# A decode attention block with an MLP on one core: the stream of keys and values issued by GpSimd instead of SyncE

## The chip, the core and the metric

The kernel runs on one core of a Trainium2 chip. A core has TensorE (PE) for matrix products, VectorE (DVE), ScalarE (ACT), GpSimd (POOL), and SyncE (SP), which computes nothing and here issues transfers. Each engine has its own list of instructions; semaphores order them against each other and against the 16 DMA engines that move data between HBM and the on-chip memory (SBUF). The metric is the device time of one execution in microseconds (us), the median over runs; lower is better.

## The reference

One token for each of B = 4 sequences. Block A is attention against a cache of 4096 positions, 32 heads of 128 dimensions; block B is a small MLP. Both take the layer-normed input, and both results are added to `x`:

```python
xn = _layernorm(x)
# A: q = xn @ wq; B=4, H=32, Sk=4096, Dh=128
scores = jnp.einsum("bhqd,bhkd->bhqk", q, k_cache) * (Dh ** -0.5)
p = _softmax(scores, axis=-1)
o = jnp.einsum("bhqk,bhkd->bhqd", p, v_cache)      # then o @ wo
# B: with one position the spatial shifts give zeros, so x1 = xn
h2 = _gelu(_layernorm(x1) @ w3) @ w4
return x + A(xn) + (x1 + h2)
```

All data are float32. The key cache and the value cache have 4 * 32 * 4096 * 128 numbers each, 268 MB each; every one is used once.

## The kernel before

**Tiles.** The 128 pairs (sequence, head) are handled in `NJ = 32` groups of four. One group's keys are one tile of 128 partitions x 16384 floats, 8,388,608 bytes: partition p holds 128 consecutive positions of one head, which is one contiguous run of 64 KB in HBM. Values have the same form. There are two tiles for keys (`ks[0]`, `ks[1]`, used in turn) and a single one for values (`vs`); together they take most of SBUF. They also serve other data before and after the loop: `vs` holds `w3` and scratch at the start and `w4` at the end, `ks[1]` holds `wq` at the start, `ks[0]` the last group's values, and `ks[1]` `wo` at the end.

**The three loops.** They run at the same time, one on each engine, and are tied by semaphores.

- DVE, L309 to L338: for each group, wait for its keys, multiply the tile with the query (L329), add up over the 128 dimensions (L330), in two halves of 64 columns, then take the maximum (L335 to L337). After each half it adds 1 to `summed`, so group j is through with its keys at `summed` = 2j + 2.
- ACT, L343 to L356: exponentials of the scores (L348), two copies out of PSUM (L353, L355). The second copy adds 1 to `done`; after that the group's values are no longer needed.
- PE, L375 to L394: wait for the values, multiply them with the exponentials (L382), then two small products (L387, L389).

**The transfers.** `load` (L164) issues a transfer on an engine's list, SP unless told otherwise, after waiting for what frees its target. In program order SP has: `w3`, `wq`, the first keys; keys 1 once the query product has read `wq` (L275); values 0 once three steps of the preamble are through (L276); keys 2 in two halves as the first keys are used up (L277); then in turn values j + 1 after `done` = j + 1 and keys j + 2 after `summed` (L279 to L282); at the end the last values, `w4` (L284), and `wo` in seven pieces (L285 to L292). SP waits in this order, so a transfer is never issued ahead of the one before it on the list. All of them go into one hardware queue (q1 in the profile).

**Handing over a landing.** A transfer adds 16 to its semaphore: `k0`, `k1` or `landed`. The loops' bodies are the same code in every pass, so the reader waits for 16 and takes 16 off again (`take`, L294):

```python
def take(engine, sem, n=1):
    engine.wait_ge(sems[sem], n)
    engine.sem_inc(sems[sem], -n)
```

Keys 2 come in two halves, which would add 16 twice; they land on `half0` and `half1`, and GpSimd waits for both and adds 16 to `k0` (L301, L302). Beside that GpSimd does small work: constants at the start (L185 to L196), clearing `pw` (L265), preparing `g4` near the end (L303, L304), and clearing the semaphores.

**The end.** The last values, `w4` and the pieces of `wo` have semaphores of their own, for which PE waits directly (L399, L402, L415, L433). `wo`'s pieces get smaller (rows of 32, 16, 8, 4, 2 and twice 1 KB per partition), so that PE has little left when the last lands. SP and ACT store the two halves of the result (L441).

Of the kernel before, what the change touches and what calls it, by code (L numbers as in the profile page):

```python
# [88 lines left out]
def decode_block(ctx: ExitStack, tc: tile.TileContext, x, k, v, wq, wo, w3, w4, out):  # L89
    nc = tc.nc  # L90
    B, H, S, DH = k.shape
# [3 lines left out]
    NF = F // P  # L95
# [6 lines left out]
    WC = H * DH // P  # L102
    LAST = NJ - 1

    def sb(name, *shape):
        return nc.alloc_sbuf_tensor(name, [P, *shape], F32).ap()
# [4 lines left out]
    ks = [sb(f"ks{n}", R * DH) for n in range(2)]  # L111
    vs = sb("vs", R * DH)
# [10 lines left out]
    gT = sb("gT", NF, B)  # L123
# [17 lines left out]
    kf = k.rearrange("b h s d -> (b h s d)")  # L141
    vf = v.rearrange("b h s d -> (b h s d)")

    def rows(flat, j):
        n = G * S * DH
        return flat[j * n:(j + 1) * n].rearrange("(p n) -> p n", p=P)

    def blocks4(start, stop, w, m, src):

        for t in range(4):  # L150
            i = nc.tensor.matmul(total[32 * t:32 * t + m, :], w, src[:, P * t:P * t + P], start=start, stop=stop)  # L151
        return i

    do = Steps(nc)
    wo_sems = [nc.alloc_semaphore(f"wo{n}") for n in range(7)]
    sems = {n: nc.alloc_semaphore(n) for n in (
        "x", "w3", "wq", "k0", "k1", "landed", "last", "w4", "go", "pv", "copied", "poz",
        "half0", "half1", "nm", "dve", "summed", "expd", "done", "bye", "out")}
    wo_sb = ks[LAST % 2].rearrange("p (c n) -> p c n", c=WC)
    wo_cuts = ((0, 16), (16, 24), (24, 28), (28, 30), (30, WC - 1))  # L160
    w4_sb = vs[:, :NF * D].rearrange("p (m n) -> p m n", m=NF)
    g4 = vs[:, NF * D:NF * D + 4 * 32].rearrange("p (m i) -> p m i", m=4)

    def load(o, i, sem, by, *after, queue="SP"):  # L164
        return do(queue, lambda e: e.dma_start(o, i), *after, done=(sems[sem], 16, by))
# [22 lines left out]
        out=ident, in_=ident, compare_op=ALU.not_equal, fill=1.0, base=0, pattern=[[-1, P]],  # L188
# [42 lines left out]
    total_ok = do("PE", lambda e: blocks4(False, False, ident[:B, 0:32], 32, xn))  # L231
# [4 lines left out]
    for c in range(NC):  # L236
        for t in range(4):
            up = lambda e: e.matmul(y[32 * t:32 * t + 32, :FT], x1nT[:, c, :], w3_sb[:, c, t * FT:(t + 1) * FT],
                                    start=(c == 0), stop=(c == NC - 1))
            d = do("PE", up)  # L240
# [3 lines left out]
    d = do("DVE", lambda e: e.tensor_mul(u, hs, hs), a)  # L244
    d = do("DVE", lambda e: e.tensor_scalar(u, u, GELU_B, 1.0, op0=ALU.mult, op1=ALU.add), d)
    d = do("DVE", lambda e: e.tensor_mul(u, u, hs), d)
    a = do("ACT", lambda e: e.activation(th, u, AF.Tanh, scale=GELU_A), d)
    d = do("DVE", lambda e: e.tensor_scalar(th, th, 1.0, 0.5, op0=ALU.add, op1=ALU.mult), a)
    d = do("DVE", lambda e: e.tensor_mul(hs, hs, th), d)
    d = do("DVE", lambda e: e.transpose(gt, hs), d)  # L250
    gT_ok = do("DVE", lambda e: e.tensor_copy(gT, gt.rearrange("p (m i) -> p m i", i=32)[:, :, 0:B]), d)
# [4 lines left out]
    for c in range(NC):  # L256
        for n in range(2):
            for h in range(G):
                q = lambda e: e.matmul(pq[n][HP * h:HP * h + HP, :], xnT[:, c, :], wq_h[:, c, n, h],
                                       start=(c == 0), stop=(c == NC - 1))  # L260
                pq_ok = do("PE", q)
    for n in range(2):
        a = do("ACT", lambda e: e.mul(pw_row[:, n * 4 * DH:(n + 1) * 4 * DH], pq[n], DH ** -0.5), pq_ok)  # L263
    d = do("DVE", lambda e: e.transpose(wide, pw_row), a)  # L264
    pw_ok = do("POOL", lambda e: e.memset(pw, 0.0), d)  # L265
    qT_ok = do("DVE", lambda e: e.tensor_copy(
        qT.rearrange("p (b i) n -> p b i n", b=B),
        wide.rearrange("p (i n m) -> p m i n", n=DH // HP, m=32)[:, 0:B]), d)
# [3 lines left out]
    SUMMED = [(sems["summed"], 2 * j + 2) for j in range(NJ)]  # L272
    DONE = [(sems["done"], j + 1) for j in range(NJ)]
    HALF = R * DH // 2
    load(ks[1], rows(kf, 1), "k1", None, pq_ok)  # L275
    load(vs, rows(vf, 0), "landed", None, gT_ok, qT_ok, total_ok)  # L276
    parts = [load(ks[0][:, n:n + HALF], rows(kf, 2)[:, n:n + HALF], f"half{i}", 16, (sems["summed"], i + 1))  # L277
             for i, n in enumerate((0, HALF))]
    for j in range(LAST - 1):  # L279
        if j > 0:  # L280
            load(ks[j % 2], rows(kf, j + 2), f"k{j % 2}", None, SUMMED[j])
        load(vs, rows(vf, j + 1), "landed", None, DONE[j])  # L282
    last_in = load(ks[(LAST - 1) % 2], rows(vf, LAST), "last", 16, SUMMED[LAST - 1])
    w4_in = load(w4_sb, w4.rearrange("(p m) n -> p m n", m=NF), "w4", 16, DONE[LAST - 1])  # L284
    do.wait("SP", [SUMMED[LAST]])  # L285
    wo_r = wo.rearrange("(p c) n -> p c n", c=WC)
    for (c0, c1), sem in zip(wo_cuts, wo_sems):
        nc.sync.dma_start(wo_sb[:, c0:c1], wo_r[:, c0:c1]).then_inc(sem, 16)  # L288
    half = D // 2
    for n, sem in enumerate(wo_sems[-2:]):  # L290
        n *= half
        nc.sync.dma_start(wo_sb[:, WC - 1, n:n + half], wo_r[:, WC - 1, n:n + half]).then_inc(sem, 16)  # L292

    def take(engine, sem, n=1):  # L294

        engine.wait_ge(sems[sem], n)
        engine.sem_inc(sems[sem], -n)  # L297


    nc.gpsimd.sem_inc(sems["expd"], 2)  # L300
    do.wait("POOL", parts)  # L301
    nc.gpsimd.sem_inc(sems["k0"], 16)  # L302
    d = do("POOL", lambda e: e.memset(g4, 0.0), DONE[LAST - 1])  # L303
    g4_ok = do("POOL", lambda e: e.tensor_copy(g4[:, :, 0:B], gT[:, 0:4, :]), d, gT_ok)  # L304


    do.wait("DVE", [qT_ok])
# [1 line left out]
    with nc.Fori(0, NJ // 2, engines=OrderedEngineSet([DVE]), head_slot={DVE: 192}) as j:  # L309
        e, n = nc.vector, 0  # L310
# [8 lines left out]
        for s in range(2):  # L319
# [14 lines left out]
            rm, nm = small[:, s, 0:1], small[:, s, 1:2]  # L334
# [8 lines left out]
    with nc.Fori(0, NJ // 2, engines=OrderedEngineSet([ACT]), head_slot={ACT: 160}) as j:  # L343
        for s in range(2):
            take(nc.scalar, "nm")
            for h in range(G):
                hp = slice(HP * h, HP * h + HP)
                i = nc.scalar.activation(  # L348
                    pw[hp, :, 4 * h:4 * h + 4], sc[s][hp, :].rearrange("p (g w) -> p g w", w=4), AF.Exp,
                    bias=small[hp, s, 1:2], scale=1.0, accum_out=rs[hp, h:h + 1])  # L350
# [45 lines left out]
    for b in range(B - 1):  # L396
        d = do("PE", lambda e: e.matmul(xb[:, b, :], lts[:, b].rearrange("p h q -> p (h q)"), sel, start=True, stop=True),
               LTS[b])
# [4 lines left out]
    for m in range(NF):  # L403
        t, g, n = (m, g4[:, m, :], 32) if m < 4 else (m % 4, gT[:, m, :], B)
        nc.tensor.matmul(y[32 * t:32 * t + n, :], g, w4_sb[:, m, :], start=(m < 4), stop=False)
    d = do("PE", lambda e: e.matmul(xb[:, B - 1, :], lts[:, B - 1].rearrange("p h q -> p (h q)"), sel, start=True,
                                    stop=True), LTS[B - 1])
# [6 lines left out]
    for (c0, c1), sem in zip(wo_cuts, wo_sems):  # L414
        do.wait("PE", [(sem, 16)])  # L415
        for c in range(c0, c1):
            if c < 24:
                t = (c + 2) % 4
                i = nc.tensor.matmul(y[32 * t:32 * t + B, :], X[:, c, :], wo_sb[:, c], start=False, stop=(c >= 20))
            else:  # L420
                i = blocks4(False, False, X[:, c, :], B, wo_sb[:, c])
        d = do("PE", lambda e: i)
# [8 lines left out]
    for t in range(4):  # L431
        q = slice(32 * t, 32 * t + B)
        do.wait("PE", [(wo_sems[5 + t // 2], 16)])  # L433
        d = do("PE", lambda e: e.matmul(total[q, :], X[:, WC - 1, :], wo_sb[:, WC - 1, P * t:P * t + P],  # L434
                                        start=False, stop=True))
# [42 lines left out]
```

## Time and profile before

| what | value |
|---|---|
| median of 3 runs | 1303.03 us (1302.62 to 1303.13) |
| span of the profiled execution, first to last instruction | 1301.2 us |
| DVE, PE, ACT, POOL busy | 1164.4, 370.9, 93.6, 2.5 us |
| transfers of keys, of values | 33 issues (one in halves), 32 issues |

The profile is that of one execution, and its times are counted from the first instruction. The 1.8 us between span and median lie outside the instructions. A "busy" engine is one with an instruction running. For DMA the page gives, in 40 slices of the span, the mean busy share of the 16 DMA engines and what they moved, and for each queue the time its packets took as a share of 16 engines' span. "SPq" is an instruction of SP that issues a transfer; its time is that of issuing alone. A wait put down to "DVEq L297" is one that ended with the engine's own `take`, which follows a landing or another engine's signal.

### The profile page before, as it was taken

What the parts mean: (1) busy time and instruction counts of PE and PEld (TensorE: products, weight loads), DVE (VectorE), ACT (ScalarE), POOL (GpSimd) and SP (SyncE); (2) the same over time, 40 slices, a digit from 0 to 9 for tenths busy, and PEclk for the clock granted to TensorE, in tenths of its full rate; (3) what the DMA queues carried; (4) which work ended last, traced back from release to release, by engine and by line L of the source; (5) the groups of instructions that cost most, each with busy time, mean ns of one, the idle gap of its engine ahead of it and who ended that gap; (6) DMA issues with size and microseconds to landing.
All of it is one profiled execution on the core that took longest, in us unless ns stands there. A gap on an engine that the chain in (4) does not pass through costs nothing. (4 is left out here: it accounts for less than half of the span.)

```text
span 1301.2 us, 6686 instructions
## 1 busy us (share of the span) xinstructions
PE 370.9 (29%) x2652; PEld 132.4 (10%) x2652; DVE 1164.4 (89%) x323; ACT 93.6 (7%) x332; POOL 2.5 (0%) x14
## 2 busy tenths in 40 slices
PE   3221233321233321233331133332123332123338
PEld 1000111100011110011110011110001110001112
DVE  3499999999999999999999999999999999999990
ACT  1000000000000000000000000000000000000001
POOL 0000000000000000000000000000000000000000
PEclk9655666655666665666665666665666665566668
DMA  9999999999999999999999999999999999999998
GB/s 404 446 422 448 425 441 427 433 435 425 445 423 445 425 443 425 433 435 427 443 423 445 425 443 427 435 433 429 439 423 447 423 443 427 439 429 433 435 423 372
DMA packets 10830, 561.08 MB, mean 431 GB/s; under 512 B 1212, under 2 KB 1476, under 8 KB 1736
## 3 DMA queue, kind: packets, MB, share of 16 engines
q1 hardware_dynamic: 10808, 561.00, 99.7%
q8 instruction: 3, 0.05, 0.0%
q14 instruction: 3, 0.02, 0.0%
q10 hardware_dynamic: 16, 0.01, 0.0%
HBM read 561.00 MB, written 0.01 MB: 431 GB/s over the span
## 5 line engine op out<-in xcount | busy, mean ns | idle before, releaser
L329 DVE TENSOR_TENSOR ks<-ks,qb 128x8192 f32<-128x8192 f32 x64 | 556.3, 8692 | 59.2 <-DVEq L297 54.2
L330 DVE TENSOR_REDUCE sc<-ks 128x64 f32<-128x8192 f32 x64 | 555.9, 8686 | 2.2
L382 PE MATMUL pv<-vs,pw 128*32 128x512 f32 x1984 | 285.6, 740 | 869.7 <-PEq L297 869.7
L382 PEld LDWEIGHTS pv<-vs,pw 128*32 128x32 f32 x1984 | 78.5, 133 | 1052.2 <-issue 1052.2
L353 ACT COPY os<-pv 128x512 f32<-128x512 f32 x32 | 18.8, 586 | 827.7 <-ACTq L297 827.7
L348 ACT ACTIVATE pw<-sc,small 32x128 f32<-32x128 f32 x128 | 50.9, 398 | 275.2 <-ACTq L297 274.0
L387 PE MATMUL poz<-sel,os 128*128 128x4 f32 x256 | 32.8, 252 | 28.0 <-PEq L297 28.0
L387 PEld LDWEIGHTS poz<-sel,os 128*128 128x128 f32 x256 | 31.0, 191 | 56.1 <-issue 56.1
L348 ACT ACTIVATION_READ_ACCUMULATOR pw<-sc,small 32x1 f32 x128 | 23.5, 184 | 0.0
L436 DVE COPY os<-total 4x128 f32<-4x128 f32 x2 | 0.6, 282 | 15.0 <-PE total L434 15.0
L335 DVE TENSOR_REDUCE small<-sc 128x1 f32<-128x128 f32 x32 | 9.2, 286 | 4.7
L363 DVE RECIPROCAL rz<-oz 128x96 f32<-128x96 f32 (+1 forms) x2 | 1.1, 553 | 13.6 <-ACT oz L355 13.5
L389 PE MATMUL poz<-rs,ones 128*128 128x4 f32 x64 | 11.7, 253 | 0.0
L321 DVE STREAM_TRANSPOSE qb<-qg 128x128 f32<-128x128 f32 x32 | 10.0, 311 | 1.1
L264 DVE STREAM_TRANSPOSE vs<-pw 128x1024 f32<-128x1024 f32 x1 | 1.2, 1245 | 10.4 <-ACT pw L263 10.4
L320 DVE COPY qg<-qT 128x4 f32 x32 | 5.4, 170 | 5.1 <-issue 4.7
L389 PEld LDWEIGHTS poz<-rs,ones 128*128 128x128 f32 x64 | 9.7, 192 | 0.0
L382 PE MATMUL pv<-ks,pw 128*32 128x512 f32 x64 | 9.5, 757 | 0.0
L202 DVE TENSOR_REDUCE lns<-vs 4x1 f32<-4x512 f32 x1 | 0.7, 674 | 9.5 <-DMA vs<-in_A_x_dram 9.5
L355 ACT COPY oz<-poz 128x8 f32 x32 | 5.3, 166 | 50.8 <-ACTq L297 50.8
L215 PE MATMUL pt<-vs,pw 4*128 4x4 f32 x16 | 4.0, 372 | 16.4 <-DVE pw L209 16.4
L336 DVE STREAM_TRANSPOSE tr<-small 128x32 f32<-128x32 f32 x32 | 6.8, 212 | 1.1
(75 smaller groups left out, 78.4 us busy)
## 6 DMA issues: line engine op xcount, KB each, us to landing
ks<-in_A_k_cache_dram SPq DMA_DIRECT2D x2, 4096.0 KB, 26.9
vs<-in_B_w_dram SPq DMA_DIRECT2D x2, 3584.0 KB, 14.1
ks<-in_A_wo_dram SPq DMA_DIRECT2D x1, 4096.0 KB, 21.8
ks<-in_A_wo_dram SPq DMA_DIRECT2D x1, 2048.0 KB, 26.3
ks<-in_A_wo_dram SPq DMA_DIRECT2D x1, 1024.0 KB, 28.3
ks<-in_A_wo_dram SPq DMA_DIRECT2D x1, 512.0 KB, 29.1
ks<-in_A_k_cache_dram SPq DMA_DIRECT2D x31, 42.2
vs<-in_A_v_cache_dram SPq DMA_DIRECT2D x31, 26.8
```

Of the source, the lines that this page charges most:

```text
L320: step(e.tensor_copy(qg, pairs[:, s, bass.ds(j, 1)].rearrange("p o n -> p (o n)")))
L321: step(e.transpose(qb.rearrange("p (n m) -> p n m", m=HP), qg.unsqueeze(2).to_broadcast([P, DH // HP, HP])))
L329: step(e.tensor_tensor(out=kt, in0=kt, in1=qb.unsqueeze(1).to_broadcast([P, w, DH]), op=ALU.mult))
L330: step(e.reduce_sum(sc[s][:, c:c + w], kt, axis=AX.X))
L335: step(e.reduce_max(rm, sc[s], axis=AX.X))
L336: step(e.transpose(tr[s], rm.to_broadcast([P, HP])))
L348: i = nc.scalar.activation(pw[hp, :, 4 * h:4 * h + 4], sc[s][hp, :].rearrange("p (g w) -> p g w", w=4), AF.Exp, bias=small[hp, s, 1:2], sc ...
L353: nc.scalar.copy(os, pv.rearrange("p (m d) -> p m d", m=4)).then_inc(sems["copied"], 1)
L355: nc.scalar.copy(ozs[:, s, :, bass.ds(j, 1)].rearrange("p n o h -> p n (o h)"), poz[:, 0:2 * G].rearrange("p (n h) -> p n h", n=2)).then_i ...
L382: i = nc.tensor.matmul(pv[32 * t:32 * t + 32, :], pw[:, g, :], vt[:, 4 * g:4 * g + 4, :], start=(g < 4), stop=(g >= NG - 4))
L387: nc.tensor.matmul(poz[:, 0:G], os[:, m, :], sel.rearrange("p (h m) -> p m h", m=4)[:, m, 0:G], start=(m == 0), stop=(m == 3))
L389: nc.tensor.matmul(poz[:, G:2 * G], ones.to_broadcast([P, P]), rs, start=True, stop=True).then_inc(sems["poz"], 1)
```

## The change

Every transfer behind the first keys moves from SP's list to GpSimd's. SP issues `w3`, `wq` and keys 0 as before, and from then on only waits for landings and passes them on: `stream` issues on GpSimd with the new semaphores `dk0`, `dk1`, `dlanded`, on which nothing is ever taken off; `tell` makes SP wait until such a semaphore has reached 16 times the number of landings so far, and add 16 to the old `k0`, `k1` or `landed`. DVE's and PE's loops are unchanged and still take from the old ones. Keys 2 are two issues on one semaphore and one `tell` for both, which replaces `half0`, `half1` and GpSimd's wait. The last values, `w4` and `wo` are issued by GpSimd too, and PE waits for them directly as before. GpSimd's two instructions for `g4` stand between `w4` and `wo` now.

```diff
+    nc.gpsimd.sem_inc(sems["expd"], 2)
+    told = {"k0": 0, "k1": 0, "landed": 0}
+
+    def stream(o, i, sem, *after):
+        do.wait("POOL", after)
+        nc.gpsimd.dma_start(o, i).then_inc(sems["d" + sem], 16)
+
+    def tell(sem, n=1):
+        told[sem] += n
+        nc.sync.wait_ge(sems["d" + sem], 16 * told[sem])
+        nc.sync.sem_inc(sems[sem], 16)
+
-    load(ks[1], rows(kf, 1), "k1", None, pq_ok)
-    load(vs, rows(vf, 0), "landed", None, gT_ok, qT_ok, total_ok)
-    parts = [load(ks[0][:, n:n + HALF], rows(kf, 2)[:, n:n + HALF], f"half{i}", 16, (sems["summed"], i + 1))
-             for i, n in enumerate((0, HALF))]
+    stream(ks[1], rows(kf, 1), "k1", pq_ok)
+    stream(vs, rows(vf, 0), "landed", gT_ok, qT_ok, total_ok)
+    for i, n in enumerate((0, HALF)):
+        stream(ks[0][:, n:n + HALF], rows(kf, 2)[:, n:n + HALF], "k0", (sems["summed"], i + 1))
+    for sem in ("k1", "landed"):
+        tell(sem)
+    tell("k0", 2)
     for j in range(LAST - 1):
         if j > 0:
-            load(ks[j % 2], rows(kf, j + 2), f"k{j % 2}", None, SUMMED[j])
-        load(vs, rows(vf, j + 1), "landed", None, DONE[j])
-    last_in = load(ks[(LAST - 1) % 2], rows(vf, LAST), "last", 16, SUMMED[LAST - 1])
-    w4_in = load(w4_sb, w4.rearrange("(p m) n -> p m n", m=NF), "w4", 16, DONE[LAST - 1])
-    do.wait("SP", [SUMMED[LAST]])
+            stream(ks[j % 2], rows(kf, j + 2), f"k{j % 2}", SUMMED[j])
+            tell(f"k{j % 2}")
+        stream(vs, rows(vf, j + 1), "landed", DONE[j])
+        if j < LAST - 2:
+            tell("landed")
+    tell("landed")
+    last_in = load(ks[(LAST - 1) % 2], rows(vf, LAST), "last", 16, SUMMED[LAST - 1], queue="POOL")
+    w4_in = load(w4_sb, w4.rearrange("(p m) n -> p m n", m=NF), "w4", 16, DONE[LAST - 1], queue="POOL")
+    d = do("POOL", lambda e: e.memset(g4, 0.0), DONE[LAST - 1])
+    g4_ok = do("POOL", lambda e: e.tensor_copy(g4[:, :, 0:B], gT[:, 0:4, :]), d, gT_ok)
+    do.wait("POOL", [SUMMED[LAST]])
...
-        nc.sync.dma_start(wo_sb[:, c0:c1], wo_r[:, c0:c1]).then_inc(sem, 16)
+        nc.gpsimd.dma_start(wo_sb[:, c0:c1], wo_r[:, c0:c1]).then_inc(sem, 16)
...
-    nc.gpsimd.sem_inc(sems["expd"], 2)
-    do.wait("POOL", parts)
-    nc.gpsimd.sem_inc(sems["k0"], 16)
```

What this does to the lists of instructions shows best at two places. The first is the start of the stream. Before, it stands on SP's list, right behind the three transfers of the preamble (a row is a line of the kernel, an operation, target and source, size and the semaphores waited for; nPE, nDVE and nPOOL count steps of those engines):

```order
L165 DMA vs<-in_B_w_dram 128x7168
L165 DMA ks<-in_A_wq_dram 128x16384
L165 DMA ks<-in_A_k_cache_dram 128x16384
L181 UNCONDITIONAL_BRANCH
L165 DMA ks<-in_A_k_cache_dram 128x16384 [waits barrier_Pool_Activation_PE_DVE_SP_release,nPE]
L165 DMA vs<-in_A_v_cache_dram 128x16384 [waits nDVE]
L165 DMA ks<-in_A_k_cache_dram 128x8192 [waits summed] x2
L165 DMA vs<-in_A_v_cache_dram 128x16384 [waits done]
```

Now the same transfers stand on POOL's list, behind its own small work:

```order
L194 MEMSET rs 128x4
L195 MEMSET ones 128x1
L196 MEMSET eps 128x1
L265 MEMSET pw 128x1024 [waits nDVE]
L280 DMA ks<-in_A_k_cache_dram 128x16384 [waits nPE]
L280 DMA vs<-in_A_v_cache_dram 128x16384 [waits nDVE]
L280 DMA ks<-in_A_k_cache_dram 128x8192 [waits summed] x2
L280 DMA vs<-in_A_v_cache_dram 128x16384 [waits done]
```

The transfers keep their order and their waits, but keys 1 come behind L265, which waits for a later step of DVE than keys 1 themselves need.

The second place is the end, the last values, `w4` and `wo`. Before, on SP:

```order
L165 DMA ks<-in_A_v_cache_dram 128x16384 [waits summed]
L165 DMA vs<-in_B_w_dram 128x7168 [waits done]
L288 DMA ks<-in_A_wo_dram 128x8192 [waits summed]
L288 DMA ks<-in_A_wo_dram 128x4096
L288 DMA ks<-in_A_wo_dram 128x2048
L288 DMA ks<-in_A_wo_dram 128x1024
L288 DMA ks<-in_A_wo_dram 128x512
L292 DMA ks<-in_A_wo_dram 128x256 x2
L441 DMA out_dram<-os 4x256 [waits nACT,nDVE]
```

Now, on POOL:

```order
L165 DMA ks<-in_A_v_cache_dram 128x16384 [waits summed]
L165 DMA vs<-in_B_w_dram 128x7168 [waits done]
L304 MEMSET vs 128x128
L305 COPY vs<-gT 128x4x4 [waits nPOOL]
L309 DMA ks<-in_A_wo_dram 128x8192 [waits summed]
L309 DMA ks<-in_A_wo_dram 128x4096
L309 DMA ks<-in_A_wo_dram 128x2048
L309 DMA ks<-in_A_wo_dram 128x1024
L309 DMA ks<-in_A_wo_dram 128x512
L313 DMA ks<-in_A_wo_dram 128x256 x2
```

The two instructions for `g4` now stand in the same list as the transfers; SP keeps the store of its half of the result alone.

More of the change, by code (lines that the diff above doesn't have):

```diff
@@ L157, in decode_block @@
         "x", "w3", "wq", "k0", "k1", "landed", "last", "w4", "go", "pv", "copied", "poz",
-        "half0", "half1", "nm", "dve", "summed", "expd", "done", "bye", "out")}
+        "dk0", "dk1", "dlanded", "nm", "dve", "summed", "expd", "done", "bye", "out")}
     wo_sb = ks[LAST % 2].rearrange("p (c n) -> p c n", c=WC)
@@ L291, in decode_block @@
         n *= half
-        nc.sync.dma_start(wo_sb[:, WC - 1, n:n + half], wo_r[:, WC - 1, n:n + half]).then_inc(sem, 16)
+        nc.gpsimd.dma_start(wo_sb[:, WC - 1, n:n + half], wo_r[:, WC - 1, n:n + half]).then_inc(sem, 16)
     def take(engine, sem, n=1):
@@ L297, in take @@
         engine.sem_inc(sems[sem], -n)
-    nc.gpsimd.sem_inc(sems["expd"], 2)
-    do.wait("POOL", parts)
-    nc.gpsimd.sem_inc(sems["k0"], 16)
-    d = do("POOL", lambda e: e.memset(g4, 0.0), DONE[LAST - 1])
-    g4_ok = do("POOL", lambda e: e.tensor_copy(g4[:, :, 0:B], gT[:, 0:4, :]), d, gT_ok)
     do.wait("DVE", [qT_ok])
```

## The prediction

> **What bounds the kernel now.** I read the head of the page first, then the DMA lines, then the stretches of the span, and last the order in time around a few landings. On the head of the page DVE looks like the bound; the DMA lines say otherwise:
>
> ```profile
> PE 370.9 (29%) x2652; PEld 132.4 (10%) x2652; DVE 1164.4 (89%) x323; ACT 93.6 (7%) x332; POOL 2.5 (0%) x14
> DMA  9999999999999999999999999999999999999998
> q1 hardware_dynamic: 10808, 561.00, 99.7%
> ```
>
> DVE is busy 89% of the span and waits now and then; the 16 DMA engines are busy in every slice, and the packets of SP's queue alone fill 99.7% of 16 engines' span. The stretches (span, busy times, granted clock, DMA share, GB/s) show the same rate from end to end:
>
> ```profile
> 46.00:100.00 54.00, 9.39 (x64) 2.57 (x64) 47.94 (x12) 2.01 (x9) 0.00 (x0) 0.55 0.99 428
> 100.00:660.00 560.00, 148.66 (x1046) 53.47 (x1046) 534.74 (x135) 40.62 (x150) 0.00 (x0) 0.61 1.00 434
> 660.00:1220.00 560.00, 152.19 (x1080) 53.96 (x1084) 520.36 (x130) 37.95 (x140) 0.00 (x0) 0.62 1.00 433
> 1297.00:1301.20 4.20, 2.44 (x61) 1.12 (x52) 0.56 (x2) 0.52 (x2) 0.00 (x0) 1.00 0.17 58
> ```
>
> The order in time gives the exact beat. These are the first use of keys 0, and then, near the end, DVE starting on keys (L329) and PE on values (L382) right after their landings, with SP's issues between:
>
> ```profile
> 51.71 8.69 DVE L329 TENSOR_TENSOR ks<-ks,qb 128x8192 f32<-128x8192 f32 x1 [5.53 <-DVEq L297]
> ...
> 1185.21 0.33 SPq L165 DMA_DIRECT2D vs<-in_A_v_cache_dram  x1
> 1189.88 0.33 SPq L165 DMA_DIRECT2D ks<-in_A_k_cache_dram  x1
> 1193.52 8.69 DVE L329 TENSOR_TENSOR ks<-ks,qb 128x8192 f32<-128x8192 f32 x1 [2.00 <-DVEq L297]
> 1212.88 9.65 PE L382 MATMUL pv<-vs,pw 128*32 128x512 f32 x64 [28.05 <-PEq L297]
> 1225.03 0.33 SPq L165 DMA_DIRECT2D vs<-in_A_v_cache_dram  x1
> 1228.57 0.33 SPq L165 DMA_DIRECT2D ks<-in_A_v_cache_dram  x1
> 1232.22 8.69 DVE L329 TENSOR_TENSOR ks<-ks,qb 128x8192 f32<-128x8192 f32 x1 [2.38 <-DVEq L297]
> ```
>
> From keys 0 (51.71) to keys 31 (1232.22) lie 61 transfers, keys 1 to 31 and values 0 to 29. That is 1180.51 / 61 = 19.35 us each, and 1193.52 to 1212.88 to 1232.22 is 19.36 and 19.34. So no transfer of the loop lost any time: 8,388,608 bytes in 19.35 us are 433.5 GB/s, all through. The kernel is one unbroken stream of 561 MB, with about 2 us ahead of it and 2 us behind. DVE needs about 36.4 us a group (1164.4 / 32) against 38.7 for two transfers; PE and ACT need less.
>
> What the stream does next is decided by how early a transfer is issued:
>
> ```profile
> ks<-in_A_k_cache_dram SPq DMA_DIRECT2D x31, 42.2
> vs<-in_A_v_cache_dram SPq DMA_DIRECT2D x31, 26.8
> ```
>
> Keys are issued 42.2 us ahead of landing and values 26.8 (medians). With 19.35 of its own, a values transfer stands 7.4 us in the queue behind other bytes, a keys transfer 22.9. In the rows above, the values issued at 1185.21 go behind keys that land at about 1193.5: 8.3 us of cover.
>
> **The change, part by part.** Removed: 70 or so issues on SP and GpSimd's wait for two halves. Moved: the same transfers, in the same order, behind the same waits, to GpSimd. Added: a wait and an increment on SP between each landing and its reader, and the preparation of transfers by GpSimd instead of SP's hardware queue. Anything that only delays an issue is free until the cover is used up.
>
> *The rate (the term that matters): taken as 0.* No row shows a transfer issued by GpSimd, so the value must be bounded. The same DMA engines move the same rows of 64 KB between the same memories. Downwards, what is left to gain is the 0.3% the queue doesn't fill (3.9 us) and whatever the engines lose at each row. Pieces of `wo` show that loss; PE starts on the one with 16 KB rows, on the one with 8 KB rows, and at the end on the last pieces as they land:
>
> ```profile
> 1293.99 1.90 PE L419 MATMUL y<-ks,X 128*4 128x512 f32 x16 [1.20 <-DMA ks<-in_A_wo_dram]
> 1296.49 1.06 PE L151 MATMUL total<-ks,X 128*4 128x128 f32 x32 [0.61 <-DMA ks<-in_A_wo_dram]
> ...
> 1298.74 0.71 PE L434 MATMUL total<-ks,X 128*4 128x128 f32 x8
> ```
>
> The stream behind keys 0 runs from 51.71 to 1298.74, 1247 us, so 1% of its rate is 12.5 us. The piece with 8 KB rows has 1,048,576 bytes in 2.50 us, where the stream's rate gives 2.42: 0.08 us over 8 rows per DMA engine, some 10 ns a row. A 64 KB transfer has 8 rows per DMA engine too, so losing nothing at a row would save 0.08 us of 19.35, 64 times: 5 us. Together with the gap, the low end is about 1303 - 6 = 1297. Upwards: should GpSimd cut the 64 KB rows, each cut costs those 10 ns again. Two pieces: 64 * 0.08 = 5 us, 1308. Four: 15 us, 1318. Rows of 8 KB throughout: 64 * 7 * 0.08 = 36 us, 1339. I take 0, since the nearest rows are the 61 transfers themselves, which are uniform.
>
> *The issue itself: 0, hidden.* An issue takes SP 0.33 us. A microsecond or two more per issue lies under the 7.4 us of the values' cover and the 22.9 of the keys'. Without cover it would cost 31 us for each microsecond, since values are issued 31 times in the loop. The Trainium skill, "DMA: Bandwidth & Descriptors", section "Specifications", gives about 1 us to the first byte for a transfer from GpSimd against about 0.6 for one from SyncE; by that the 0.4 us are hidden too, and the sum stays the same. No run here shows it yet.
>
> *The relay on SP: 0.* A landing reaches its reader one wait and one increment later, by SP's shortest rows some tenths of a microsecond. Behind SP's wait stand only the next landings, in the order of the stream, so none is held up by a later one. The readers start that much later, so `summed` and `done` come that much later, out of the same 7.4 us of cover. At the end nothing is relayed: PE waits for the last values, `w4` and `wo` directly.
>
> *The start: 0.* Keys 1 now come behind POOL's clearing of `pw`:
>
> ```profile
> 41.79 0.33 SPq L165 DMA_DIRECT2D ks<-in_A_k_cache_dram  x1
> 44.19 1.05 DVE L266 COPY qT<-vs 128x128 f32<-128x128 f32 x1
> 44.21 0.95 POOL L265 MEMSET pw<- 128x1024 f32 x1 [40.20 <-DVE vs L264]
> 45.27 0.33 SPq L165 DMA_DIRECT2D vs<-in_A_v_cache_dram  x1
> ```
>
> So they are issued at 45.2 instead of 41.8; keys 0 land at 51.7. The cover shrinks from 9.9 to 6.5 us, and values 0 follow at once. If GpSimd's first issue took 6 us more than SP's, the stream would begin to stand still; bounds 0 to 3 us, I take 0.
>
> *The end: +0.5.* `w4` is issued at 1263.16, `wo` from 1267.27 on, with one piece after the other:
>
> ```profile
> 1251.58 9.08 PE L382 MATMUL pv<-vs,pw 128*32 128x512 f32 x64 [26.93 <-PEq L297]
> ...
> 1263.16 0.33 SPq L165 DMA_DIRECT2D vs<-in_B_w_dram  x1
> 1263.19 0.20 POOL L303 MEMSET vs<- 128x128 f32 x1 [1218.03 <-ACT oz L355]
> 1263.46 0.20 POOL L304 COPY vs<-gT 128x16 f32<-128x16 f32 x1
> 1267.27 2.50 SPq L288 DMA_DIRECT2D ks<-in_A_wo_dram  x5
> 1269.82 0.90 SPq L292 DMA_DIRECT2D ks<-in_A_wo_dram  x2
> ...
> 1282.81 1.84 PE L405 MATMUL y<-vs 128*32 128x512 f32 x8
> ```
>
> SP needs 3.45 us for the seven. Should GpSimd need three times as long, the last would be issued at 1278. Behind the values that PE starts on at 1251.58 come the last values, `w4` and `wo`'s first piece, 16.3 MB, which keep the DMA engines busy to about 1289. The two instructions for `g4` (0.20 us each) stand behind `w4`'s issue and are needed only at 1282.81 (L405). What can show is the last landing itself, if its completion takes longer from GpSimd's queue: bounds -0.5 to +2, I take +0.5.
>
> Sum: 1301.2 + 0.5 = 1301.7 for the span, and with the 1.8 us around it **1303.5 us**.
>
> **The rivals.** (1) *Faster: the DMA engines lose less between rows or transfers* when GpSimd prepares them. For it: 0.3% unfilled and some 10 ns a row. Against it: 61 transfers at 19.35 us leave little. It gives 1297 to 1300, say 1299. Beside it stands the fit in the same page of the Trainium skill, section "Anatomy of one DMA — SWDGE (gpsimd) path", with 436 GB/s for the part that grows with size: an estimate by it is 0.6% above the 433.5 here, some 7 us less, 1296.
>
> (2) *Slower: the rate falls* because rows are cut, or one of the 16 DMA engines gets its work later than the others and every transfer waits for it. For it: there is no slack in the rate at all; every loss shows in full. Against it: same engines, same bytes. It decides from the first nanosecond: rows in two, 1308; in four, 1318; 8 KB, 1339. The table in the same page, section "Measured (HBM→SBUF, 128 partitions, SWDGE, issued from GpSimd)", has 425 GB/s at its largest size, 2% under the stream here, an estimate of 1328; it disagrees with the fit of rival 1, and no row here decides between them.
>
> (3) *Slower: values are issued too late.* The point from which it counts is 7 to 8 us of delay between `done` and the first byte. One thing in the trace could be that long: an instruction of DVE, if GpSimd could not prepare a transfer beside it.
>
> ```profile
> 178.73 8.69 DVE L329 TENSOR_TENSOR ks<-ks,qb 128x8192 f32<-128x8192 f32 x1
> 180.11 0.17 ACT L355 COPY oz<-poz 128x8 f32 x1 [1.58 <-ACTq L297]
> 180.30 0.33 SPq L165 DMA_DIRECT2D vs<-in_A_v_cache_dram  x1
> ```
>
> These values would be prepared only at 187.42, 7.1 us late; with a microsecond for the issue the stream stops for about half a microsecond, and if every group were hit so, 31 * 0.5 = 15 us, 1319. Against it: most issues fall beside L330 or into gaps. The Trainium skill, "SBUF — State Buffer", section "Who interferes with whom", has a rule against such changes: GpSimd's preparation of transfers waits for DVE's copies in a two-port mode. It clears L329's and L330's kinds of instruction of that, which leaves DVE's copies here, at most 1.05 us long; by the rule the sum stays.
>
> (4) *Slower by a one-off*: the first issue or the end outside the cover, +3 to +5, 1307.
>
> **How the numbers follow.** My forecast, 1300.4 to 1305.6 by itself: 0.34. Rival 1: 0.24. Rival 2: 0.24. Rival 3: 0.10. Rival 4: 0.08. A measurement of this kernel tells about 0.2% (2.6 us) from no change. So faster 0.24, the same 0.34, slower 0.24 + 0.10 + 0.08 = 0.42. The range 1297 to 1326 leaves out the fastest 0.05, and of rivals 2 and 3 what lies above it, rows cut finer than in four or whole microseconds lost per group, 0.13.
>
> **What would show it.** Right: on the new queue, packets of 64 KB (its megabytes over its packets near 52 KB, as on q1 now), values landing 19.35 us apart, DMA share 1.00 from 100 to 1220. Rival 1: the spacing under 19.3. Rival 2: the spacing over 19.4 with the share still at 1.00, or the share under 1.00 with an even spacing. Rival 3: the median from issue to landing of values near 20 us and a DMA share under 1.00 in the loop. Rival 4: a gap before keys 1 or a later start of PE's last steps, with the loop's beat kept. The forecast is wrong if the beat moves by more than 0.04 us.

## The result and the profile after

| | median | lowest to highest | ratio to before, 95% interval |
|---|---|---|---|
| before (8 runs) | 1303.02 us | 1302.57 to 1303.43 | |
| changed (8 runs) | 1306.38 us | 1303.71 to 1306.82 | 1.0024 (1.0015 to 1.0033) |

The change costs 3.4 us, 0.24%. The profiled execution is the fastest of the eight (1303.71 us, span 1302.3); the other seven took 1306.0 to 1306.8. So its trace shows the loss in small, and the first experiment below was made to get a trace of a usual execution.

First what did not change. From the page of the changed kernel, POOL's issues, the queues and the transfers with their median times to landing; from the stretches of the span, the two long ones (busy time of PE, PEld, DVE, ACT and POOL, granted clock, DMA share, GB/s):

```profile
L280 POOL DMA_DIRECT2D vs<-in_A_v_cache_dram x31 | 16.4, 528 | 916.7 <-ACT oz L370 916.7
...
q0 software_dynamic: 10112, 540.55, 96.0%
q1 hardware_dynamic: 440, 20.45, 3.7%
...
vs<-in_A_v_cache_dram POOLq DMA_DIRECT2D x31, 26.7
ks<-in_A_k_cache_dram POOLq DMA_DIRECT2D x30, 41.9
```

```profile
100.00:660.00 560.00, 149.63 (x1070) 53.81 (x1062) 535.89 (x135) 40.64 (x150) 15.82 (x30) 0.62 1.00 433
660.00:1220.00 560.00, 150.08 (x1076) 53.36 (x1080) 520.40 (x129) 37.91 (x140) 14.78 (x28) 0.61 1.00 433
```

GpSimd's queue q0 carries 540.55 MB in 10112 packets, 53.5 KB each (51.9 KB on q1 before): the 64 KB rows are not cut. The rate is 433 GB/s with a DMA share of 1.00, where it was 434 and 433 before. An issue keeps POOL for 0.53 us where SP needed 0.33, and medians from issue to landing moved by 0.1 and 0.3 us.

Now the order in time at the start, where something did change. These rows of the kernel before stand against the rows of the changed kernel below: the issues of keys 1 (only in the second), values 1 and keys 3, DVE's first start on keys 0, and PE's starts on values 1 and values 2.

```profile
102.33 0.33 SPq L165 DMA_DIRECT2D vs<-in_A_v_cache_dram  x1
123.12 0.33 SPq L165 DMA_DIRECT2D ks<-in_A_k_cache_dram  x1
129.20 8.78 PE L382 MATMUL pv<-vs,pw 128*32 128x512 f32 x64 [27.27 <-PEq L297]
167.90 9.90 PE L382 MATMUL pv<-vs,pw 128*32 128x512 f32 x64 [27.80 <-PEq L297]
```

```profile
44.90 0.67 POOL L280 DMA_DIRECT2D ks<-in_A_k_cache_dram  x1
54.09 8.69 DVE L344 TENSOR_TENSOR ks<-ks,qb 128x8192 f32<-128x8192 f32 x1 [8.12 <-DVEq L318]
105.33 0.53 POOL L280 DMA_DIRECT2D vs<-in_A_v_cache_dram  x1 [15.39 <-ACT oz L370]
125.78 0.53 POOL L280 DMA_DIRECT2D ks<-in_A_k_cache_dram  x1 [19.92 <-DVEq L348]
129.39 8.66 PE L397 MATMUL pv<-vs,pw 128*32 128x512 f32 x64 [24.72 <-PEq L318]
169.04 9.31 PE L397 MATMUL pv<-vs,pw 128*32 128x512 f32 x64 [28.86 <-PEq L318]
```

Keys 0 were issued as before, at about 1.7 us, yet they land later. This is their time from issue to landing, in the kernel before and then in the changed one:

```profile
ks<-in_A_k_cache_dram SPq DMA_DIRECT2D x1, 49.9
```

```profile
ks<-in_A_k_cache_dram SPq DMA_DIRECT2D x1, 52.3
```

So DVE starts on them at 54.09 instead of 51.71. Keys 3 follow at 125.78 instead of 123.12, since their tile is free that much later. Values 1 are nearly on time (129.39 against 129.20). But between values 1 and values 2, two transfers later, lie 39.65 us instead of 38.70. From there the beat is the old one. The changed kernel's PE on values 30 near the end (1251.58 before):

```profile
1252.87 3.69 PE L397 MATMUL pv<-vs,pw 128*32 128x512 f32 x20 [27.59 <-PEq L318]
```

From 169.04 to 1252.87 are 56 transfers, 19.35 us each. Values 2 are 1.14 us late, values 30 1.29, and the span is 1.1 us longer. One hiccup of the stream around 128 us makes nearly the whole difference of this execution, and it begins with keys 0 landing late.

### The profile page after: what moved, and what is told of

It is laid out like the page before. It is cut to its first block, busy times and chain, and to the rows that moved or that the text cites. A ratio compares the mean times of both kernels' runs of the same rounds, so it can differ in the third digit from the quotient of the medians.

```text
span 1302.3 us, 6747 instructions
## 1 busy us (share of the span) xinstructions
PE 366.9 (28%) x2652; PEld 131.6 (10%) x2652; DVE 1164.5 (89%) x323; ACT 93.5 (7%) x332; POOL 40.5 (3%) x86
## 3 DMA queue, kind: packets, MB, share of 16 engines
q0 software_dynamic: 10112, 540.55, 96.0%
## 5 line engine op out<-in xcount | busy, mean ns | idle before, releaser
L397 PE MATMUL pv<-vs,pw 128*32 128x512 f32 x1984 | 282.5, 733 | 873.6 <-PEq L318 873.6
L280 POOL DMA_DIRECT2D vs<-in_A_v_cache_dram x31 | 16.4, 528 | 916.7 <-ACT oz L370 916.7
L280 POOL DMA_DIRECT2D ks<-in_A_k_cache_dram x32 | 17.0, 532 | 231.5 <-DVEq L348 231.5
## 6 DMA issues: line engine op xcount, KB each, us to landing
vs<-in_A_v_cache_dram POOLq DMA_DIRECT2D x31, 26.7
```

What stands on the lines that cost most here:

```text
L280: nc.gpsimd.dma_start(o, i).then_inc(sems["d" + sem], 16)
L397: i = nc.tensor.matmul(pv[32 * t:32 * t + 32, :], pw[:, g, :], vt[:, 4 * g:4 * g + 4, :], start=(g < 4), stop=(g >= NG - 4))
```

## The experiments

Theory A was formed from these rows: keys 0 (still on SP's queue) and keys 1 (now on GpSimd's) are served by the DMA engines in turn, so keys 0 land late, DVE starts late, and the first transfers that wait for DVE are issued too late to keep the stream unbroken. Its rivals: (B) each transfer from GpSimd costs a little; (C) SP's relay; (D) the sharing itself loses time, DVE's start does not matter; (E) only GpSimd's queue takes turns with SP's.

### The changed kernel again

> The changed kernel once more, for a profile of one of its usual executions (1306 us; the profiled one took 1303.71 and its span is 1302.3). Theory A, the start: keys 0 (SP's queue) and keys 1 (GpSimd's) share the DMA engines, so keys 0 land at 54 instead of 51.7 us, DVE starts 2.4 us late, and keys 3 are issued so close to the end of values 1 that the DMA engines run dry there, once. Then the spacing of landings is 19.35 us from keys 4 on, as before, and some 3 us are missing between values 1 and keys 3 (19.9 instead of 19.35 in the trace at hand, 22 to 23 here). Theory B, the beat: every transfer prepared by GpSimd costs a little more; then the spacing is 19.39 to 19.41 all through the loop (64 x 0.05 = 3 us). Theory C, the relay: the landings are as before and PE and DVE start later at the end. Time for all: 1306.4.

Measured: 1306.51 us, ratio 1.0026 (1.0015 to 1.0037). The profiled execution took 1306.58, span 1305.0. Its order in time, with the same places as above:

```profile
43.77 0.67 POOL L280 DMA_DIRECT2D ks<-in_A_k_cache_dram  x1
56.51 8.69 DVE L344 TENSOR_TENSOR ks<-ks,qb 128x8192 f32<-128x8192 f32 x1 [11.66 <-DVEq L318]
107.01 0.53 POOL L280 DMA_DIRECT2D vs<-in_A_v_cache_dram  x1 [14.65 <-ACT oz L370]
128.19 0.53 POOL L280 DMA_DIRECT2D ks<-in_A_k_cache_dram  x1 [20.65 <-DVEq L348]
132.20 9.43 PE L397 MATMUL pv<-vs,pw 128*32 128x512 f32 x64 [25.85 <-PEq L318]
171.71 8.45 PE L397 MATMUL pv<-vs,pw 128*32 128x512 f32 x64 [27.95 <-PEq L318]
...
1255.51 4.97 PE L397 MATMUL pv<-vs,pw 128*32 128x512 f32 x24 [26.74 <-PEq L318]
```

DVE starts 4.80 us late, and values 1 are late as well: they were issued at 107.01 instead of 102.33, and PE takes them up 3.0 us late; values 2 are 3.81 late. So the stream is broken twice here, by 3.0 us ahead of the landing of values 1 and by another 0.8 behind it. From 171.71 to 1255.51 the 56 transfers take 19.35 us each again. Theory B is out: the beat is the same.

The two amounts by which DVE starts late, 2.38 and 4.80 us, are one and two times 2.42 us, which is a 64 KB row at the beat of 8 rows per DMA engine (19.35 / 8). The packets that start around the landing of keys 0 show what came in between. Before, in the stretch from 49.0 to 51.2 us, 32 packets start on q1:

```profile
DMA packets 32, 1.05 MB, mean 477 GB/s; under 512 B 16, under 2 KB 16, under 8 KB 16
```

Sixteen of them are rows of keys 1. The other sixteen are under 512 B; they come behind the last rows of keys 0, as many as there are DMA engines, and the landing is counted after them, at 51.6. In the profiled execution of the change, the one with DVE at 54.09, these packets start from 49.0 to 51.2 and from 51.2 to 54.0 us:

```profile
q0 software_dynamic: 16, 1.05, 111.2%
...
q0 software_dynamic: 16, 1.05, 86.5%
q1 hardware_dynamic: 16, 0.00, 0.3%
```

No row of keys 0 (q1) starts in either stretch: all had started by 49.0, as before. Only the sixteen small packets start late, behind the sixteen rows of keys 1 (q0). So the keys themselves were in place in time, and their landing was signalled a row late. In the usual execution the stretches from 49.0 to 51.2, 51.2 to 54.0 and 53.6 to 56.4 us have

```profile
q0 software_dynamic: 13, 0.85, 89.3%
q1 hardware_dynamic: 3, 0.20, 20.6%
...
q1 hardware_dynamic: 13, 0.00, 0.3%
...
q1 hardware_dynamic: 3, 0.00, 0.1%
```

Here keys 1 were issued 1.1 us earlier (43.77 against 44.90), and three of the last rows of keys 0 themselves come behind rows of keys 1, and their small packets behind another row each. That makes two rows, and DVE waits for the last of the sixteen.

The Trainium skill, "DMA: Bandwidth & Descriptors", section "Queues, rings and completion order", has the rule for this: a DMA engine goes round the queues that have work for it, switching after a whole packet. The trace agrees, with steps of 2.4 us, where the packet is one row of 64 KB.

### GpSimd from values 1 on

Keys 1, values 0 and keys 2 go back to SP and land as before the change:

```diff
-    stream(ks[1], rows(kf, 1), "k1", pq_ok)
-    stream(vs, rows(vf, 0), "landed", gT_ok, qT_ok, total_ok)
-    for i, n in enumerate((0, HALF)):
-        stream(ks[0][:, n:n + HALF], rows(kf, 2)[:, n:n + HALF], "k0", (sems["summed"], i + 1))
-    for sem in ("k1", "landed"):
-        tell(sem)
-    tell("k0", 2)
+    load(ks[1], rows(kf, 1), "k1", None, pq_ok)
+    load(vs, rows(vf, 0), "landed", None, gT_ok, qT_ok, total_ok)
+    parts = [load(ks[0][:, n:n + HALF], rows(kf, 2)[:, n:n + HALF], f"half{i}", 16, (sems["summed"], i + 1))
+             for i, n in enumerate((0, HALF))]
+    do.wait("SP", parts)
+    nc.sync.sem_inc(sems["k0"], 16)
```

> Keys 1, values 0 and both halves of keys 2 are issued by SP as before the change and land directly; GpSimd issues from values 1 on, and SP relays from there. Theory A: keys 0 land at 51.7 again, DVE starts there, keys 3 are issued at 123.5 as before, 4 us ahead of the end of values 1: no gap, 1303.0 to 1303.6. Keys 2 share the DMA engines with values 1 and land some 5 us later, which DVE does not need before 123. Theory B: 60 of 64 transfers keep their price, 1306. Theory C (relay): 1306.

Measured: 1303.20 us, ratio 1.0002 (0.9992 to 1.0012). Its order in time and its two queues:

```profile
51.70 8.69 DVE L343 TENSOR_TENSOR ks<-ks,qb 128x8192 f32<-128x8192 f32 x1 [6.98 <-DVEq L317]
123.40 0.53 POOL L280 DMA_DIRECT2D ks<-in_A_k_cache_dram  x1 [19.69 <-DVEq L347]
167.90 8.64 PE L396 MATMUL pv<-vs,pw 128*32 128x512 f32 x64 [27.35 <-PEq L317]
```

```profile
q0 software_dynamic: 9536, 515.38, 91.5%
q1 hardware_dynamic: 1016, 45.62, 8.2%
```

515 of 561 MB still come through GpSimd with SP's relay, keys 3 are issued by GpSimd 0.28 us later than by SP, and the loss is gone: DVE starts at 51.70 and values 2 are on the spot at 167.90. The two queues meet here as well, keys 2 on q1 with values 1 on q0, and the halves of keys 2 land in 29.3 us (median of the two) instead of 26.9; but DVE begins keys 2 only at 124.81, and no time is lost. The whole price lies in where the stream changes queues.

### The relay alone

SP issues everything, on the new semaphores, and GpSimd does the passing on:

```diff
-        do.wait("POOL", after)
-        nc.gpsimd.dma_start(o, i).then_inc(sems["d" + sem], 16)
+        do.wait("SP", after)
+        nc.sync.dma_start(o, i).then_inc(sems["d" + sem], 16)
...
-        nc.sync.wait_ge(sems["d" + sem], 16 * told[sem])
-        nc.sync.sem_inc(sems[sem], 16)
+        nc.gpsimd.wait_ge(sems["d" + sem], 16 * told[sem])
+        nc.gpsimd.sem_inc(sems[sem], 16)
```

> SP issues everything as before the change, but the transfers land on the new semaphores and GpSimd passes each landing on: the relay without the move of the issues. Theories A and B: 1303.0 to 1303.3, the relay is hidden by the cover. Theory C: 1306.

Measured: 1302.75 us, ratio 1.0000 (0.9990 to 1.0009). The relay is free with GpSimd passing on, and the version with the later switch, where SP passes on the loop's landings from values 1 on, stands at 1.0002. Theory C is out.

### Everything on GpSimd's queue

```diff
-    w3_in = load(w3_sb, w3.rearrange("(p c) f -> p c f", c=NC), "w3", 16)
-    wq_in = load(wq_sb, wq.rearrange("(p c) n -> p c n", c=NC), "wq", 16)
-    k_in = {0: load(ks[0], rows(kf, 0), "k0", 16)}
+    w3_in = load(w3_sb, w3.rearrange("(p c) f -> p c f", c=NC), "w3", 16, queue="POOL")
+    wq_in = load(wq_sb, wq.rearrange("(p c) n -> p c n", c=NC), "wq", 16, queue="POOL")
+    k_in = {0: load(ks[0], rows(kf, 0), "first", 16, queue="POOL")}
...
+    nc.sync.wait_ge(sems["first"], 16)
+    nc.sync.sem_inc(sems["k0"], 16)
```

> GpSimd issues w3, wq and keys 0 too, so that one queue carries all and keys 0 no longer share the DMA engines with keys 1. Theory A: keys 0 land 19.35 us after wq, DVE starts then, no gap at keys 3; what is left is a later first byte at the start (0 to 1.5 us): 1303.0 to 1304.5. Theory B: 67 of 67 transfers dearer, 1306.5. Theory C: 1306.

Measured: 1336.88 us, ratio 1.0260 (1.0242 to 1.0277); all three theories missed. POOL's first instruction behind the preamble's transfers, and keys 1:

```profile
52.37 0.20 POOL L185 MEMSET vs<- 128x128 f32 x1 [49.40 <-POOLq L181]
...
82.34 0.55 POOL L280 DMA_DIRECT2D ks<-in_A_k_cache_dram  x1
```

The three transfers of the preamble stand ahead of a point where all engines meet (L181). With them on its own list, GpSimd passes that point only at 52.37 us, when keys 0 have just landed (issued at 2.44, 49.2 us from issue to landing); with them on SP's it went on at 2.88. That GpSimd waits there for its own transfers is read from these two times alone. The small layers, which had run beside the transfers, ran behind them, and keys 1 were issued at 82.34 instead of 41.79. The stream stood still for some 30 us, and the median is 34 us up. The experiment says nothing on theory A; it shows another place where the issuing engine matters.

### DVE made late, keys 0 not

A sum that nothing uses keeps DVE busy past the landing of keys 0, once in the kernel before and once in the version with the later switch:

```diff
+    busy = lts[:, 0].rearrange("p h q -> p (h q)").unsqueeze(1).to_broadcast([P, 76, P])
+    do("DVE", lambda e: e.reduce_sum(rz[:, 0:76], busy, axis=AX.X), qT_ok, x1nT_ok)
     do.wait("DVE", [qT_ok])
```

> The kernel before, with a sum of 10 us that nothing uses put on DVE ahead of its loop, so that DVE starts on keys 0 at about 56.5 us instead of 51.7, as in the usual execution of the change (56.51), while keys 0 still land at 51.6. Theory A (DVE's late start makes the issue of values 1 and keys 3 late): keys 3 are issued 4.8 us later than at 123.1, at 127.9, with values 1 ending on the first DMA engine at 127.4. With SP's issue that costs 1 to 2.5 us once: 1304 to 1305.5. If DVE's start does not matter (theory D: it is the sharing of the DMA engines itself that loses time): 1303.0.

> The version that switched to GpSimd at values 1 (1303.2), with the same sum on DVE ahead of its loop: GpSimd issues values 1 and keys 3, no keys 0 are shared, and DVE starts at 56.5. Theory A: the whole loss of the change comes back, 1305.5 to 1306.8, and what it has over the kernel before with the same sum (0.5 to 1.5 us) is the price of GpSimd's issue and SP's relay where they have no cover. Theory D: 1303.2.

Measured: 1304.10 us, ratio 1.0009 (0.9999 to 1.0019), with SP's issues; 1305.30 us, 1.0018 (1.0009 to 1.0028), with GpSimd's. Here are DVE's start, the issue of keys 3 and PE on values 2, of the first and then of the second:

```profile
55.27 8.69 DVE L331 TENSOR_TENSOR ks<-ks,qb 128x8192 f32<-128x8192 f32 x1
126.69 0.33 SPq L165 DMA_DIRECT2D ks<-in_A_k_cache_dram  x1
168.88 8.80 PE L384 MATMUL pv<-vs,pw 128*32 128x512 f32 x64 [27.26 <-PEq L297]
```

```profile
54.94 8.69 DVE L345 TENSOR_TENSOR ks<-ks,qb 128x8192 f32<-128x8192 f32 x1
126.64 0.54 POOL L280 DMA_DIRECT2D ks<-in_A_k_cache_dram  x1 [21.22 <-DVEq L349]
168.99 10.01 PE L398 MATMUL pv<-vs,pw 128*32 128x512 f32 x64 [27.97 <-PEq L317]
```

DVE started 3.2 to 3.6 us late rather than the 4.8 intended, and that alone, with every transfer of the start on one queue, makes values 2 late by 1.0 and 1.1 us. Theory D, which has no loss here, is out by these rows; the time alone would not do with SP's issues, since its interval reaches 0.9999. GpSimd's version is 1.2 us above SP's by the medians, though both scatter (1303.4 to 1306.4, and 1304.2 to 1306.6), and the early rows differ by 0.1 us only. The two versions also differ in the relay and in the second queue from values 1 on, so what GpSimd's issue costs without cover is not settled; these runs leave anything from 0.1 to 1.2 us. The expectation for GpSimd's version, 1305.5 to 1306.8, was missed by 0.2.

### Two hardware queues, no GpSimd

The kernel before, with keys 1, values 0 and keys 2 issued by ACT:

```diff
-    load(ks[1], rows(kf, 1), "k1", None, pq_ok)
-    load(vs, rows(vf, 0), "landed", None, gT_ok, qT_ok, total_ok)
+    load(ks[1], rows(kf, 1), "k1", None, pq_ok, queue="ACT")
+    load(vs, rows(vf, 0), "landed", None, gT_ok, qT_ok, total_ok, queue="ACT")
-    parts = [load(ks[0][:, n:n + HALF], rows(kf, 2)[:, n:n + HALF], f"half{i}", 16, (sems["summed"], i + 1))
+    parts = [load(ks[0][:, n:n + HALF], rows(kf, 2)[:, n:n + HALF], f"half{i}", 16, (sems["summed"], i + 1), queue="ACT")
```

> The kernel before with keys 1, values 0 and keys 2 issued by ACT ahead of its loop, all else by SP: two hardware queues at the place of the switch, and nothing by GpSimd. Theory A: keys 1 go out at 43 and share the DMA engines with keys 0, which then land 2 or 3 packets of 2.42 us late, at 56 to 59; DVE starts so late and the loss is like the change's, 1304.5 to 1308. If only GpSimd's queue takes turns with SP's (theory E): 1303.0.

Measured: 1308.43 us, ratio 1.0047 (1.0033 to 1.0062). Its order in time:

```profile
41.57 0.36 ACTq L165 DMA_DIRECT2D ks<-in_A_k_cache_dram  x1
58.93 8.69 DVE L329 TENSOR_TENSOR ks<-ks,qb 128x8192 f32<-128x8192 f32 x1 [12.98 <-DVEq L297]
109.17 0.33 SPq L165 DMA_DIRECT2D vs<-in_A_v_cache_dram  x1
130.35 0.33 SPq L165 DMA_DIRECT2D ks<-in_A_k_cache_dram  x1
```

Keys 1 were issued at 41.57 us, as early as SP did before, and DVE starts 7.22 us late, three rows of 2.42. The loss is larger than the change's, and the time 0.4 us above the expected range. So it is the second queue, and not GpSimd, that delays keys 0; theory E is out.

### Keys 1 held back

More clearings of `pw`, each 0.95 us, between GpSimd's preamble and its first transfer (n = 1, 2, 3):

```diff
     pw_ok = do("POOL", lambda e: e.memset(pw, 0.0), d)
+    for _ in range(n):
+        pw_ok = do("POOL", lambda e: e.memset(pw, 0.0), pw_ok)
```

> The change with GpSimd's clearing of pw done three times more (0.95 us each), so that keys 1 are issued some 2.9 us later, at 46.7 to 47.8, and reach the DMA engines when these are on their last packet of keys 0. Theory A: keys 0 land at 51.6 to 54, DVE starts 0 to 2.4 us late: 1303.1 to 1304.2, a delay that makes the kernel faster. Theory B (a price per transfer) or D: 1306.4. If keys 1 come after the DMA engines run dry (from 49.9 on): up to 1305, with a gap in front of keys 1.

> The change with one clearing of pw more on GpSimd, so that keys 1 are issued about 1 us later (45.9 instead of 44.9). In the run with three more (issue at 48.05, 1304.8) DVE started at 51.96 but the DMA engines ran dry between 49.9 and 51. Theory A: keys 1 reach the DMA engines at about 48.5, when those that are ahead are on their last packet of keys 0 and those behind still have one to go: keys 0 land one packet of 2.42 us late, at 54, DVE starts at 54.1, no gap before keys 1: 1303.7 to 1304.8. If the issue time of keys 1 does not set the loss: 1306.4.

> Two clearings more, keys 1 issued at about 47.0. Theory A: keys 1 reach the DMA engines at about 49.6, when all are on their last packet of keys 0 or just through: DVE starts at 51.7 and next to no gap before keys 1: 1303.0 to 1303.8, the best of this row of four (0, 1, 2, 3 clearings more). If the issue time of keys 1 does not set the loss: 1306.4.

The profiled executions of n = 3, 1 and 2, one after the other:

```profile
48.05 0.67 POOL L282 DMA_DIRECT2D ks<-in_A_k_cache_dram  x1
51.96 8.69 DVE L346 TENSOR_TENSOR ks<-ks,qb 128x8192 f32<-128x8192 f32 x1 [5.50 <-DVEq L320]
130.89 9.69 PE L399 MATMUL pv<-vs,pw 128*32 128x512 f32 x64 [28.06 <-PEq L320]
```

```profile
46.35 0.67 POOL L282 DMA_DIRECT2D ks<-in_A_k_cache_dram  x1
54.17 8.69 DVE L346 TENSOR_TENSOR ks<-ks,qb 128x8192 f32<-128x8192 f32 x1 [7.39 <-DVEq L320]
```

```profile
46.18 0.67 POOL L282 DMA_DIRECT2D ks<-in_A_k_cache_dram  x1
54.20 8.69 DVE L346 TENSOR_TENSOR ks<-ks,qb 128x8192 f32<-128x8192 f32 x1 [8.60 <-DVEq L320]
```

| clearings more | keys 1 issued | DVE starts | median, us | ratio, 95% interval |
|---|---|---|---|---|
| 0 (the change again) | 43.77 | 56.51 | 1306.51 | 1.0026 (1.0015 to 1.0037) |
| 1 | 46.35 | 54.17 | 1304.59 | 1.0014 (1.0004 to 1.0023) |
| 2 | 46.18 | 54.20 | 1304.57 | 1.0015 (1.0005 to 1.0024) |
| 3 | 48.05 | 51.96 | 1304.81 | 1.0015 (1.0006 to 1.0025) |

Holding the issue back makes the kernel faster by 1.7 to 1.9 us. With n = 1 and 2 keys 0 land one row late instead of two. With n = 3 they lose next to nothing (51.96), but keys 1 come after the first DMA engines have run dry (DMA share 0.76 from 48 to 53 us, against 1.00 before), and values 1 are 1.7 us late (130.89 against 129.20). The optimum that was expected at n = 2 was not met: in the profiled execution keys 1 went out at 46.18 instead of the expected 47.0, and the moment itself moves by a microsecond between executions (43.77 and 44.90 in two of the same kernel). No setting came near the 1303.2 of the later switch, and no version here beats the kernel before beyond its interval.

## Why the prediction was right where it was, and what failed

The forecast was 1303.5 us, no change within 0.2%, with a range of 1297 to 1326 and slower as the likeliest side (0.42). The median is 1306.38, inside the range, 2.9 us above the forecast and 0.8 us above its own upper end, 1305.6. A range of 29 us makes lying inside it say little; the terms say more.

- *The rate, taken as 0:* right. 53.5 KB a packet, 19.35 us a transfer, DMA share 1.00. Rivals 1 and 2 are out, and so are the two rates that the prediction takes from the Trainium skill beside them: neither 436 nor 425 GB/s, but the 433 of SP's queue.
- *The issue, 0, hidden:* right for the loop. An issue costs POOL 0.53 us, and the version with the later switch, with 515 MB through GpSimd, stands at 1.0002. Rival 3 did not happen: values keep 26.7 us from issue to landing. (By its own figures, 7.1 + 1.0 - 7.4, its loss would have been 0.7 us a group, not a half.)
- *The relay, 0:* right (1.0000 with the relay alone, 1.0002 with SP's relay and the later switch).
- *The end, +0.5:* not settled. In the profiled execution of the change values 30 are 1.29 us late and the span 1.1 us longer, so the end adds nothing. With the later switch values 30 are on time and the span is 0.4 us longer (1301.6), near the term.
- *The start, 0, "The cover shrinks from 9.9 to 6.5 us, and values 0 follow at once":* this step failed, and with it the number. It asked whether keys 1 come too late for an unbroken stream, and they did not: 44.90 was early enough. It did not ask what keys 1 do to keys 0, which stood on another queue and were not yet through. The runs showed their landing one to two rows of 2.42 us late, DVE late by 2.4 to 4.8 us, and a price of 3.3 us (1306.51 against 1303.20 with the later switch) for a term taken as 0 with bounds of 0 to 3.
- *The cover:* the second half of the failure. The prediction used medians, 7.4 us for values and 22.9 for keys. The first ones have far less: keys 3 were issued at 123.12, and values 1, which they follow in the stream, are taken up by PE at 129.20, 6.1 us later. The median keys are issued 42.2 us ahead because later in the loop DVE waits for keys; for the first groups it is DVE that is behind. A start late by 3.6 us with SP's issues already cost values 2 about 1 us. The size does not follow from DVE's lateness alone: in the profiled executions 2.38 us cost values 2 1.14, 3.56 (SP's issues) 0.98, 4.80 cost 3.81 and 7.22 (ACT's queue) 3.86. What sets it beside the lateness stays open.

Rival 4, the one-off at +3 to +5 us (0.08), came nearest in kind and size, but for another reason: a loss that appears 75 us behind its cause. The chain is shown link by link: two queues make the landing of keys 0 late (with ACT's queue too), a late DVE makes the issues of values 1 and keys 3 late and breaks the stream (with the sum too), and without the change of queues at this place the loss is gone.

## What to carry to other kernels

Where one stream is handed from one queue to another, as here with rows of 64 KB, the end of the old queue and the beginning of the new one are served in turn. What someone is waiting for at the end of the old one is signalled late by whole rows, even where its data are already there. Change queues where nothing is waiting for the last transfer of the old one, or keep one queue for all. And read the cover of a transfer at its smallest, in the first groups, not from the median of the loop.

## What was not expected of the hardware

- 64 KB transfers issued by GpSimd run at the same beat as SP's, to 0.01 us in 19.35, beside a DVE that is busy 89% of the span.
- The landing of a transfer can be late when its data are not: in the profiled execution of the change no row of keys 0 was held up, only the sixteen small packets behind them, and DVE started 2.38 us late.
- GpSimd seems to wait for its own transfers at the point where all engines meet: 49.40 us in the version with everything on its queue, where the same transfers on SP's list held nobody up. This is one run, and the cause of the wait was not tried.
- Some experiments lose more at the end of the span than values 2 are late: with the added sum in the kernel before, values 2 are 0.98 us late, while the profiled span is 1303.6 us against 1301.2, 2.4 more. Values 30 are 0.93 us late there (1252.51 against 1251.58), so the rest is lost behind them; what adds it was not tried.
